# Attention output with the channels on the partitions: y in four column groups of TensorE, without transposes of x

## The chip, the cores and the metric

The kernel runs on one core of one Trainium2 chip. The metric is the device time of one execution, in microseconds (us). A core has TensorE (PE, matrix products), VectorE (DVE), ScalarE (ACT), GpSimd (POOL) and SyncE (SP), which here issues most of the DMA transfers. TensorE writes its products to PSUM; the other operands lie in SBUF. In a product the stationary operand (lhsT) is loaded first, the streamed one (rhs) then runs through, one column after the other, and the output has the columns of lhsT on its partitions. Everything is f32. In the trace an f32 product is two passes, each a weight load and a matmul; a transpose is one.

## The reference

Two blocks stand one behind the other: a linear attention with a decaying state (4 batches, 8 heads, 768 tokens, 48 channels a head), and a feed-forward block over the 3072 rows of 384 channels that it makes.

```python
for t in range(S):                                   # attention, per batch and head
    cur = einsum('bhd,bhe->bhde', u[None] * kt, vt)
    y[:, :, t] = einsum('bhd,bhde->bhe', rt, state + cur)
    state = w[None, :, :, None] * state + einsum('bhd,bhe->bhde', kt, vt)
...
x = y.transpose(0, 2, 1, 3).reshape(B * S, H * D)    # 3072 x 384
h = x @ w_in                                         # 384 -> 1024
e = exp(h - max(h)); sm = e / (sum(e) + 1e-09)
solu = h * sm
ln = (solu - mean) / sqrt(var + 1e-06) * g_ln
out = ln @ w_out                                     # 1024 -> 384
```

## The kernel before

The work is cut into 24 units: six chunks of 128 tokens for each of four batches, chunk by chunk, so that the four batches take turns and a unit finds the state that its batch left four units earlier. Units 0 to 3 are the first chunks and have no state yet; the last four leave none behind.

A unit passes through these functions of `direct_path`:

- `load` (L456): SP fetches k, r and v of the unit into `kpad`, `rpad` (heads padded from 48 to 64 columns) and `vt` (heads of 48 columns, tokens on the partitions; six buffers).
- `weigh` (L601): POOL weighs k into `kp`, and makes the products for the token's own term; ACT writes that term onto the diagonal of `AT`.
- `turn` (L617): TensorE transposes r and k, two heads at a time, to `rT` and `kT` (channels on the partitions, tokens as columns; head pair `a`, `HP` = 4 pairs).
- `scores` (L631): for each head 48 channels by 128 tokens against each other; the two heads of a pair stand in different halves of TensorE's rows. DVE copies what is causal into `AT` (earlier token on the partitions, later token as column).
- `finish` (L644): y of the unit into one PSUM tile `y_ps`, with the tokens on the partitions: four products `rT` by state (L652, stationary `rT`, streamed 96 columns of the state, two heads), then eight products `AT` by `vt` (L657, stationary the scores of a head, streamed its 48 columns of v). ACT copies `y_ps` to `x` (L661). Then k times v (L665) and DVE and POOL bring the state up to date.
- `turn_x` (L674): three transposes of `x`, 128 channels each, to `xt_ps`, and a copy on ACT to `xT` (L680), since the feed-forward block needs the channels on the partitions.
- `ffn_in` (L682): h in two halves of 512 columns into `h_ps` (L687, 12 passes), then max, exp, product and variance on DVE, ACT and POOL.
- `turn_ln` (L709) transposes the normed row (L715), and `ffn_out` (L721) makes the output (L726, 16 passes), which ACT copies and SP writes out.

The order of TensorE's work is written out by hand: the loop at L740 runs under a manual schedule for TensorE alone, and each iteration `i` issues, in this order, the transposes of unit i+2, those of the normed rows of unit i−8, h of unit i−5 (`LA` = 5), the scores of unit i+1, the output of unit i−8 (`LO` = 3 more), y of unit i, and the transposes of x of unit i−4. The other engines' order is the scheduler's. In the first iterations the weights are fetched as pairs of 32-bit words and converted (`convert`, L489) on ACT, DVE and POOL beside the attention. When y has run out, four iterations of the feed-forward block follow that still transpose an x, and then the last outputs.

PSUM: `psM` has four buffers of one bank, shared by all the small tiles (`y_ps`, `kv_ps`, `xt_ps` and so on); `h_ps` has one buffer of two banks, and the scores have two banks.

Of the kernel before, what the change touches and what calls it, by code (L numbers as in the profile page):

```python
# [9 lines left out]
F32 = mybir.dt.float32  # L10
# [386 lines left out]
def direct_path(  # L397
# [184 lines left out]

    def check_range():

        ok = small.tile([1, dm], F32, tag="ok", name="ok")
        ok2 = small.tile([1, dm], F32, tag="ok2", name="ok2")
# [3 lines left out]
        all_ok = small.tile([1, 1], F32, tag="all_ok", name="all_ok")  # L590
# [6 lines left out]
    def pair(t, a):  # L597
        return t[:, 2 * a : 2 * a + 2, :].rearrange("p q d -> p (q d)")
# [42 lines left out]
            nc.vector.copy_predicated(A4[:, :, q, :], later.to_broadcast([128, HP, T]), pss[q])  # L641


    def finish(i):  # L644
        b, c = units[i]
        X = live[i]
        vt, AT, St = vts[i % NV], X["AT"], states[b]
        y_ps = psM.tile([128, H, D], F32, tag="m", name="y_ps")
        first = True
        if c > 0:  # L650
            for a in range(HP):
                nc.tensor.matmul(y_ps[:, 2 * a : 2 * a + 2, :].rearrange("p q d -> p (q d)"),  # L652
                                 X["rT"][:, a, :], St[:, a].rearrange("p q d -> p (q d)"),
                                 start=first, stop=False, skip_group_check=True)
                first = False
        for h in range(H):
            nc.tensor.matmul(y_ps[:, h, :], AT[:, h, :], vt[:, h, :],  # L657
                             start=first, stop=(h == H - 1), skip_group_check=True)
            first = False
        x = X["x"] = fpool.tile([128, dm], F32, name="x", bufs=LA + 1)  # L660
        nc.scalar.copy(out=x, in_=y_ps.rearrange("p h d -> p (h d)"))  # L661
        if c < C - 1:
            kv_ps = psM.tile([128, HP, 2, D], F32, tag="m", name="kv_ps")
            for a in range(HP):
                nc.tensor.matmul(kv_ps[:, a].rearrange("p q d -> p (q d)"),  # L665
                                 pair(X["kp"], a), pair(vt, a), start=True, stop=True)
            if c > 0:
                nc.vector.tensor_add(St, kv_ps, St)
                nc.gpsimd.tensor_mul(St, St, wt)
            else:  # L670
                nc.vector.tensor_mul(St, kv_ps, wt)


    def turn_x(i):  # L674
        X = live[i]
        xt_ps = psM.tile([128, KD, 128], F32, tag="m", name="xt_ps")
        for j in range(KD):
            nc.tensor.transpose(xt_ps[:, j, :], X["x"][:, ts(j, 128)], ident)  # L678
        X["xT"] = fpool.tile([128, KD, 128], F32, name="xT")
        nc.scalar.copy(out=X["xT"], in_=xt_ps)  # L680

    def ffn_in(i):  # L682
        X = live[i]
# [55 lines left out]
    with tc.manual_schedule(engines={mybir.EngineType.PE}):  # L739
        for i in range(-2, N + LA + LO):  # L740
            j, l = i - LA, i - LA - LO
            if 0 <= i and i + 4 < N:
                load(i + 4)
            if 0 <= i + 3 and i + 3 < N and i + 3 >= 2:
                weigh(i + 3)
            if 0 <= i + 2 < N:
                turn(i + 2)
            for _ in range(count.get(i, 1)):
                if i >= -1 and todo:
                    convert(todo.pop(0))  # L750
                if ahead < len(pieces):
                    load_weights(ahead)
                    ahead += 1
            if i == 10:
                check_range()
            if 0 <= l < N and i < N + LA:
                turn_ln(l)
            if 0 <= j < N:
                ffn_in(j)
            if 0 <= i + 1 < N:  # L760
                scores(i + 1)
            if N + LA - 1 <= i < N + LA + LO - 1:
# [50 lines left out]
```

## Time and profile before

| | us |
|---|---|
| median of 3 runs | 456.85 (455.9 to 458.77) |
| the profiled execution: its time | 458.56 |
| the profiled execution: its span, first to last instruction | 456.7 |
| DMA, mean over the span | 57 GB/s |

The profile is one execution. A row such as "256.88 1.91 PE L657 MATMUL ... x16" is 16 instructions of line 657 that begin 256.88 us after the first instruction and end 1.91 us later. The ends of matmuls are modelled and reach into the start of the next, so lengths of stages are best taken from start to start. In a row of the grouped list the numbers behind the bar are the busy time, the mean of one in ns, and the time that the engine stood idle just before such an instruction, with what released it. The granted clock of TensorE was 0.985 of full speed over the span.

### The profile page before, as it was taken

The page shows a single profiled execution, that of the slowest core. Times are in us where ns is not written, and L with a number is a line of the kernel's source. Part 1 is how long each engine was busy: PE and PEld are TensorE (multiplying, and loading weights), DVE is VectorE, ACT ScalarE, POOL GpSimd, SP SyncE. Part 2 cuts the span into 40 slices and gives each one's busy share as a digit, 9 for nine tenths or more (in the row PEclk, how much of TensorE's full clock was granted, in tenths as well). Part 3 has the DMA queues.
Part 4 walks back from the last instruction along what each step waited for, and adds up shares of the span by engine and source line. Part 5 has one row for each costly group of instructions (what it writes and reads, how often), then busy time and mean ns, then how long its engine had stood idle before and what let it go on. Part 6 is the DMA issues. An engine that isn't in the chain of part 4 may idle for free.

```text
span 456.7 us, 5931 instructions
## 1 busy us (share of the span) xinstructions
PE 423.7 (93%) x2221; PEld 289.5 (63%) x2221; DVE 219.5 (48%) x386; ACT 191.2 (42%) x446; POOL 130.9 (29%) x159
## 2 busy tenths in 40 slices
PE   0399897998999999999999999999999999999995
PEld 0398875664766756757757757757756665555562
DVE  5648887987443443443443443533443233333410
ACT  1576578764524524523523523523422233332310
POOL 4447676785223223223223213200000000000000
PEclk9999799999999999999999999999999999999998
DMA  9969949142203203213213101000000000000011
GB/s 156 221 172 180 190 102 195 14 69 52 60 12 70 53 17 69 52 18 70 47 24 69 42 11 37 18 1 17 19 0 19 17 19 17 17 2 17 17 37 40
DMA packets 81587, 25.84 MB, mean 57 GB/s; under 512 B 76557, under 2 KB 79758, under 8 KB 81550
## 3 DMA queue, kind: packets, MB, share of 16 engines
q1 hardware_dynamic: 80364, 25.17, 26.9%
q10 hardware_dynamic: 1186, 0.20, 0.3%
q8 instruction: 19, 0.31, 0.3%
q14 instruction: 18, 0.15, 0.1%
HBM read 20.65 MB, written 4.72 MB: 56 GB/s over the span
## 4 chain that ended last, share of the span: by engine, by line
PE 76%; DVE 11%; ACT 5%; issue 3%; POOL 3%; DMA 1%; ACTq 0%; POOLq 0%
PE h_ps L687 24%; PE o_ps L726 23%; PE y_ps L657 8%; PE at L638 5%; PE t_ps L715 4%; PE kv_ps L665 3%; PE y_ps L652 3%; PE tk_ps L627 2%; PE tr_ps L623 2%; ACT AT L615 1%; DVE solu L697 1%; ACT e L693 1%; PE xt_ps L678 1%; DVE st L691 1%; DVE ma L504 1%
## 5 line engine op out<-in xcount | busy, mean ns | idle before, releaser
L687 PE MATMUL h_ps<-w_in_sb,xT 128*128 128x512 f32 x288 | 129.8, 600 | 2.9 <-DVE solu L697 1.9
L726 PE MATMUL o_ps<-w_out_sb,lnT 128*128 128x384 f32 x384 | 129.2, 490 | 0.0
L726 PEld LDWEIGHTS o_ps<-w_out_sb,lnT 128*128 128x128 f32 x384 | 71.5, 190 | 49.0 <-issue 2.4
L687 PEld LDWEIGHTS h_ps<-w_in_sb,xT 128*128 128x128 f32 x288 | 53.5, 192 | 62.6 <-issue 58.1
L693 ACT ACTIVATE e<-h_ps,st 128x1024 f32<-128x1024 f32 x24 | 26.7, 1113 | 110.8 <-DVE st L691 110.8
L615 ACT ACTIVATE AT<-ident,own 128x128 f32<-128x128 f32 x192 | 60.6, 391 | 10.1 <-DVE own L612 10.0
L702 POOL TENSOR_SCALAR st<-st 128x1 f32<-128x1 f32 x24 | 4.9, 205 | 200.3 <-ACT sq L701 200.2
L691 DVE TENSOR_REDUCE st<-h_ps 128x1 f32<-128x1024 f32 x24 | 29.4, 1223 | 58.9 <-PE h_ps L687 58.9
L657 PE MATMUL y_ps<-vt,AT 128*128 128x48 f32 x384 | 49.5, 285 | 0.0
L657 PEld LDWEIGHTS y_ps<-vt,AT 128*128 128x128 f32 x384 | 48.0, 203 | 0.7 <-issue 0.4
L701 ACT ACTIVATE sq<-solu,st 128x1024 f32<-128x1024 f32 x24 | 27.6, 1149 | 44.3 <-DVE st L699 44.3
L705 DVE TENSOR_SCALAR solu<-solu,st 128x1024 f32<-128x1024 f32 x24 | 21.6, 899 | 50.0 <-POOL st L704 47.5
L605 POOL TENSOR_TENSOR kp<-kpad,kdec 128x512 f32<-128x512 f32 x24 | 30.8, 1287 | 43.3 <-PE kv_ps L665 40.4
L638 PEld LDWEIGHTS at<-rT,kT 48*128 48x128 f32 x384 | 25.7, 200 | 18.0 <-issue 13.9
L641 DVE COPY_PREDICATED AT<-later,at 128x512 f32<-128x512 uint32 x48 | 32.7, 726 | 3.0 <-PE at L638 3.0
L638 PE MATMUL at<-rT,kT 48*128 48x128 f32 x384 | 31.0, 300 | 2.4 <-DVE AT L641 2.4
L612 DVE TENSOR_REDUCE own<-rku 128x8 f32<-128x384 f32 x24 | 13.1, 548 | 38.2 <-POOL rku L610 38.2
L610 POOL TENSOR_TENSOR rku<-rku,rpad 128x384 f32<-128x384 f32 x24 | 24.5, 1021 | 23.4 <-DMA rpad<-in_r_dram 22.8
L697 DVE SCALAR_TENSOR_TENSOR solu<-h_ps,st,e 128x1024 f32<-128x1024 f32 x24 | 30.8, 1283 | 0.8
L609 POOL TENSOR_TENSOR rku<-kpad,u_bc 128x384 f32<-128x384 f32 x24 | 26.2, 1093 | 8.4 <-DMA kpad<-in_k_dram 5.5
L661 ACT COPY x<-y_ps 128x384 f32<-128x384 f32 x24 | 11.4, 476 | 38.5 <-PE y_ps L657 38.5
L715 PE MATMUL t_ps<-ident,solu 128*128 128x128 f32 x192 | 25.2, 273 | 2.0 <-DVE st L699 1.9
(67 smaller groups left out, 424.2 us busy)
## 6 DMA issues: line engine op xcount, KB each, us to landing
kpad<-in_k_dram SPq DMA_DIRECT2D x24, 192.0 KB, 4.2
rpad<-in_r_dram SPq DMA_DIRECT2D x24, 192.0 KB, 4.9
vt<-in_v_dram SPq DMA_DIRECT2D x24, 192.0 KB, 3.0
out_dram<-o SPq DMA_DIRECT2D x24, 192.0 KB, 1.9
raw<-in_moe_w_in_dram SPq DMA_DIRECT2D x6, 512.0 KB, 5.2
raw<-in_moe_w_out_dram SPq DMA_DIRECT2D x8, 384.0 KB, 3.4
u_bc<-in_u_dram ACTq DMA_DIRECT2D x1, 192.0 KB, 3.7
g_sb<-in_moe_g_ln_dram ACTq DMA_DIRECT2D x1, 4.0 KB, 5.6
```

The lines of the kernel that those rows point to most:

```text
L605: nc.gpsimd.tensor_mul(kp.rearrange("p h d -> p (h d)"), kt.rearrange("p h d -> p (h d)"), kdec.rearrange("p a d -> p (a d)"))
L615: nc.scalar.activation(out=AT[:, h, :], in_=ident, func=ACT.Copy, scale=own[:, h])
L638: nc.tensor.matmul(pss[q][:, a, :], X["kT"][rows, a, :], X["rT"][rows, a, :], start=True, stop=True)
L641: nc.vector.copy_predicated(A4[:, :, q, :], later.to_broadcast([128, HP, T]), pss[q])
L657: nc.tensor.matmul(y_ps[:, h, :], AT[:, h, :], vt[:, h, :], start=first, stop=(h == H - 1), skip_group_check=True)
L687: nc.tensor.matmul(h_ps[:, ts(n, NX)], X["xT"][:, j, :], w_in_sb[:, j, ts(n, NX)], start=(j == 0), stop=(j == KD - 1))
L691: nc.vector.tensor_reduce(out=nmax, in_=h_ps, axis=AX.X, op=ALU.max, negate=True)
L693: nc.scalar.activation(out=e, in_=h_ps, func=ACT.Exp, bias=nmax, accum_out=se)
L697: nc.vector.scalar_tensor_tensor(out=solu, in0=h_ps, scalar=rs, in1=e, op0=ALU.mult, op1=ALU.mult, accum_out=tot)
L701: nc.scalar.activation(out=sq, in_=solu, func=ACT.Square, bias=nmu, accum_out=ss)
L715: nc.tensor.transpose(t_ps[:, f, :], X["solu"][:, ts(4 * g + f, 128)], ident)
L726: nc.tensor.matmul(o_ps, X["lnT"][:, f, :], w_out_sb[:, f, :], start=(f == 0), stop=(f == KF - 1))
```

## The change

y is computed with the channels on the partitions, so that it can be used by `ffn_in` as it stands. The operands change places: the state and v become the stationary side, cut into pieces of 32 channels, and `rT` and the scores the streamed side, 128 tokens at a time. The 384 channels are 12 pieces; piece `m` goes to partitions 32·(m mod 4) and on, of column block m div 4 of `y_ps`. A piece that straddles two heads of a pair (every third) is made of two products: `vt` gets 32 zero columns behind each head's 48, and each of the two products takes 32 columns of which 16 are zeros. So there are 12 products with the state and 16 with the scores, ordered so that consecutive ones go to partition groups 0, 1, 2, 3 in turn. ACT copies `y_ps` straight to `xT`, which now has six buffers; `x`, its transposes and the second copy are gone, and `turn_x` is no longer called. Four small constants get one buffer each in place of four, and POOL clears the new columns of `vt` once at the start.

```diff
-    vts = [const.tile([128, H, D], F32, name=f"vt{i}") for i in range(NV)]
+    vts = [const.tile([128, H, D + 32], F32, name=f"vt{i}") for i in range(NV)]
...
+    for vt in vts:
+        nc.gpsimd.memset(vt[:, :, D:], 0.0)
...
-    mf = small.tile([128, T], F32, tag="mf", name="mf")
+    mf = small.tile([128, T], F32, tag="mf", name="mf", bufs=1)
...
+    def parts(m):
+        a, n = divmod(m, 3)
+        at = {0: [(0, 0)], 1: [(0, 32), (1, 64)], 2: [(1, 96)]}[n]
+        return [(2 * a + q, a * 2 * (D + 32) + off) for q, off in at]
+
+    inner = [[(m,) + p for m in range(g, 12, 4) for p in parts(m)] for g in range(4)]
+    inner = [group[n] for n in range(4) for group in inner]
...
-        y_ps = psM.tile([128, H, D], F32, tag="m", name="y_ps")
-        first = True
+        vf = vt.rearrange("p h d -> p (h d)")
+        y_ps = psM.tile([128, KD, 128], F32, tag="m", name="y_ps")
+        last = {m: n for n, (m, h, at) in enumerate(inner)}
+        opened = set()
+
+        def into(m, lhsT, rhs, stop):
+            j, g = divmod(m, 4)
+            nc.tensor.matmul(y_ps[32 * g : 32 * g + 32, j, :], lhsT, rhs, start=(g not in opened),
+                             stop=stop, skip_group_check=True)
+            opened.add(g)
+
         if c > 0:
-            for a in range(HP):
-                nc.tensor.matmul(y_ps[:, 2 * a : 2 * a + 2, :].rearrange("p q d -> p (q d)"),
-                                 X["rT"][:, a, :], St[:, a].rearrange("p q d -> p (q d)"),
-                                 start=first, stop=False, skip_group_check=True)
-                first = False
-        for h in range(H):
-            nc.tensor.matmul(y_ps[:, h, :], AT[:, h, :], vt[:, h, :],
-                             start=first, stop=(h == H - 1), skip_group_check=True)
-            first = False
-        x = X["x"] = fpool.tile([128, dm], F32, name="x", bufs=LA + 1)
-        nc.scalar.copy(out=x, in_=y_ps.rearrange("p h d -> p (h d)"))
+            for m in range(12):
+                a, n = divmod(m, 3)
+                into(m, St[:, a].rearrange("p q d -> p (q d)")[:, ts(n, 32)], X["rT"][:, a, :],
+                     False)
+        for n, (m, h, at) in enumerate(inner):
+            into(m, vf[:, at : at + 32], AT[:, h, :], last[m] == n)
+        X["xT"] = fpool.tile([128, KD, 128], F32, name="xT", bufs=LA + 1)
+        nc.scalar.copy(out=X["xT"], in_=y_ps)
         if c < C - 1:
...
-                                 pair(X["kp"], a), pair(vt, a), start=True, stop=True)
+                nc.tensor.matmul(kv_ps[:, a], pair(X["kp"], a), vt[:, 2 * a : 2 * a + 2, 0:D],
+                                 start=True, stop=True)
...
-    def turn_x(i):
-        X = live[i]
-        xt_ps = psM.tile([128, KD, 128], F32, tag="m", name="xt_ps")
-        for j in range(KD):
-            nc.tensor.transpose(xt_ps[:, j, :], X["x"][:, ts(j, 128)], ident)
-        X["xT"] = fpool.tile([128, KD, 128], F32, name="xT")
-        nc.scalar.copy(out=X["xT"], in_=xt_ps)
...
-            if 0 <= j + 1 < N:
-                turn_x(j + 1)
```

More of the change, by code (lines that the diff above doesn't have):

```diff
@@ L583, in check_range @@
     def check_range():
-        ok = small.tile([1, dm], F32, tag="ok", name="ok")
-        ok2 = small.tile([1, dm], F32, tag="ok2", name="ok2")
+        ok = small.tile([1, dm], F32, tag="ok", name="ok", bufs=1)
+        ok2 = small.tile([1, dm], F32, tag="ok2", name="ok2", bufs=1)
         nc.vector.tensor_single_scalar(out=ok, in_=wrow, scalar=LOW, op=ALU.is_ge)
@@ L589, in check_range @@
         nc.vector.tensor_mul(ok, ok, ok2)
-        all_ok = small.tile([1, 1], F32, tag="all_ok", name="all_ok")
+        all_ok = small.tile([1, 1], F32, tag="all_ok", name="all_ok", bufs=1)
         nc.vector.tensor_reduce(out=all_ok, in_=ok, axis=AX.X, op=ALU.min)
@@ L664, in finish @@
             for a in range(HP):
-                nc.tensor.matmul(kv_ps[:, a].rearrange("p q d -> p (q d)"),
-                                 pair(X["kp"], a), pair(vt, a), start=True, stop=True)
+                nc.tensor.matmul(kv_ps[:, a], pair(X["kp"], a), vt[:, 2 * a : 2 * a + 2, 0:D],
+                                 start=True, stop=True)
             if c > 0:
```

## The prediction

> **What bounds the kernel now.** I read the page's first lines and slices first, then the busy time by stretches, then TensorE's timeline of one iteration.
>
> ```profile
> span 456.7 us, 5931 instructions
> PE 423.7 (93%) x2221; PEld 289.5 (63%) x2221; DVE 219.5 (48%) x386; ACT 191.2 (42%) x446; POOL 130.9 (29%) x159
> PE   0399897998999999999999999999999999999995
> ...
> ```
> ```profile
> 30.00:63.00 33.00, 30.64 (x227) 28.77 (x227) 26.14 (x41) 19.96 (x50) 21.35 (x18) 0.90 0.89 167
> 63.00:118.30 55.30, 49.71 (x276) 32.42 (x275) 45.10 (x74) 36.47 (x88) 36.20 (x38) 0.97 0.42 76
> 118.30:373.40 255.10, 255.10 (x1395) 174.64 (x1393) 106.33 (x183) 99.11 (x230) 55.20 (x72) 1.00 0.15 34
> 373.40:456.70 83.30, 76.91 (x269) 43.95 (x268) 23.98 (x43) 22.19 (x42) 3.71 (x10) 0.98 0.06 20
> ```
>
> The columns of the second fence are the stretch, its length, then the busy time of PE, weight loads, DVE, ACT and POOL. From 118.3 to 373.4 us TensorE is busy for all of the 255.10 us, while DVE has 106 and ACT 99: there every nanosecond taken off TensorE comes off the time, and every one added is paid. Between 63 and 118 us TensorE is idle for 5.6 us and DVE is busy for 45 of 55: the conversion of the weights stands beside it. After 373 us 6.4 us of TensorE are idle.
>
> One iteration of the full stretch, TensorE alone (start, duration, and how many passes; an f32 product is two passes, a transpose one):
>
> ```profile
> 249.66 1.16 PE L638 MATMUL at<-rT,kT 48*128 48x128 f32 x16
> 250.75 5.43 PE L726 MATMUL o_ps<-w_out_sb,lnT 128*128 128x384 f32 x16
> 256.01 1.03 PE L652 MATMUL y_ps<-state,rT 128*128 128x96 f32 x8
> 256.88 1.91 PE L657 MATMUL y_ps<-vt,AT 128*128 128x48 f32 x16
> 258.62 1.10 PE L665 MATMUL kv_ps<-vt,kp 128*128 128x96 f32 x8
> 259.56 0.49 PE L678 MATMUL xt_ps<-ident,x 128*128 128x128 f32 x3
> 259.89 0.60 PE L623 MATMUL tr_ps<-ident,rpad 128*128 128x128 f32 x4
> ...
> 260.76 1.04 PE L715 MATMUL t_ps<-ident,solu 128*128 128x128 f32 x8
> 261.63 5.32 PE L687 MATMUL h_ps<-w_in_sb,xT 128*128 128x512 f32 x12
> 266.88 1.16 PE L638 MATMUL at<-rT,kT 48*128 48x128 f32 x16
> ```
>
> The ends overlap the next starts (matmuls are pipelined), so I count from start to start: the iteration is 266.88 − 249.66 = 17.22 us. Of it y takes 258.62 − 256.01 = 2.61 us for 24 passes and the transposes of x 259.89 − 259.56 = 0.33 us for 3. That is the part the change replaces: 2.94 us.
>
> **What the change puts there.** Per unit with a state: 12 products of a 32-column piece of the state with rT, and 16 of a 32-column piece of vt with the scores, 28 products or 56 passes, each streaming 128 columns; they go round four column groups of 32. What one such pass costs alone the trace shows at full width: eight passes that stream 128 columns (L715) take 261.63 − 260.76 = 0.87 us, 0.109 us each. y now streams 48 columns and its 16 passes take 1.74 us, also 0.109 each, so there the 128-column weight load is the limit and not the streaming. The change exchanges a short stream and a wide load for a long stream and a narrow load; with one pass at a time it would lose: 56 × 0.109 = 6.10 us in place of 2.94. It wins only if the column groups run beside each other.
>
> No instruction of this trace has a column group. The bounds of one round of four passes are therefore 0.109 us (four at once cost what one does) and 4 × 0.109 = 0.436 us (one after the other). The nearest row is L638: there two heads stand in two row groups, and 16 passes with 128 streamed columns take 250.75 − 249.66 = 1.09 us, where one after the other they would need 16 × 0.109 = 1.74. They do run beside each other, although each head's two passes follow each other in the program. So I take the lower end: 56 / 4 = 14 rounds × 0.109 = 1.53 us.
>
> **The price of changing the grouping.** L638 also shows what entering and leaving such a grouping costs, in iterations with and without it:
>
> ```profile
> 345.03 5.32 PE L687 MATMUL h_ps<-w_in_sb,xT 128*128 128x512 f32 x12
> 350.28 1.16 PE L638 MATMUL at<-rT,kT 48*128 48x128 f32 x16
> 351.37 5.43 PE L726 MATMUL o_ps<-w_out_sb,lnT 128*128 128x384 f32 x16
> 356.63 1.03 PE L652 MATMUL y_ps<-state,rT 128*128 128x96 f32 x8
> ...
> 360.46 5.32 PE L687 MATMUL h_ps<-w_in_sb,xT 128*128 128x512 f32 x12
> 365.62 5.32 PE L726 MATMUL o_ps<-w_out_sb,lnT 128*128 128x384 f32 x16
> 370.78 1.03 PE L652 MATMUL y_ps<-state,rT 128*128 128x96 f32 x8
> ```
>
> h_ps takes 5.25 us ahead of the scores and 5.16 ahead of o_ps; o_ps takes 5.26 behind the scores and 5.16 behind h_ps: 0.10 on either side. Inside, 8 rounds × 0.109 = 0.87 leave 1.09 − 0.87 = 0.22 us. One excursion costs 0.42 us, and y has none today. It lies on TensorE, so it is paid. Bounds: 0 and twice that; I take 0.42.
>
> So y becomes 1.53 + 0.42 = 1.95 us for 2.94: 0.99 us less. Units 8 to 23 finish in the full stretch: 16 × 0.99 = **15.8 us**.
>
> **The tail.** Four iterations after the last y have a transpose of x alone:
>
> ```profile
> 386.00 0.48 ACT L680 COPY xT<-xt_ps 128x384 f32<-128x384 f32 x1
> 386.53 5.42 PE L687 MATMUL h_ps<-w_in_sb,xT 128*128 128x512 f32 x12 [0.24 <-ACT xT L680]
> 391.78 5.32 PE L726 MATMUL o_ps<-w_out_sb,lnT 128*128 128x384 f32 x16
> 396.94 0.49 PE L678 MATMUL xt_ps<-ident,x 128*128 128x128 f32 x3
> 398.54 1.98 PE L687 MATMUL h_ps<-w_in_sb,xT 128*128 128x512 f32 x4 [0.23 <-ACT xT L680]
> ```
>
> They last 398.54 − 386.53 = 12.01 us: h_ps waits for the copy L680, which stands behind other ACT work. With neither transpose nor copy there remain t_ps 0.87, h_ps 5.16 and o_ps 5.16, 11.19 us: 4 × 0.82 = **3.3 us**. What is late next there is nothing near: solu of the unit is due three iterations later.
>
> **The first 118 us.** Units 0 to 3 have no state and no transpose in their iteration: 16 passes at 0.109 = 1.74 us become 32 passes, 8 rounds, 0.87 + 0.42 = 1.29. Units 4 to 7 gain 0.99 each. In all 4 × 0.45 + 4 × 0.99 = 5.8 us less work, but the chain of waits leaves TensorE between 64 and 106 us:
>
> ```profile
> 66.19 1.35 POOL kp L605
> ...
> 71.46 2.45 ACT AT L615 x8
> ...
> 77.19 0.36 ACT xT L680
> ...
> 104.34 1.29 DVE solu L697 x2
> ```
>
> There the saved time turns into longer waits. The copies of x lie on ACT, which is on that chain, and one of two goes. Bounds 0 and 5.8; I take **2**, near the lower end, because the chain is elsewhere.
>
> **What costs nothing, and why.**
>
> ```profile
> 0.78 0.20 POOL masks.py:197 MEMSET ident<- 128x128 f32 x1 [0.29 <-POOLq L797]
> 1.65 0.42 POOL L574 MEMSET wt<- 128x384 f32 x1
> 5.41 1.58 SPq L460 DMA_DIRECT2D vt<-in_v_dram  x1
> 6.01 1.19 POOL L609 TENSOR_TENSOR rku<-kpad,u_bc 128x384 f32<-128x384 f32 x1 [3.94 <-DMA kpad<-in_k_dram]
> L661 ACT COPY x<-y_ps 128x384 f32<-128x384 f32 x24 | 11.4, 476 | 38.5 <-PE y_ps L657 38.5
> ```
>
> - Six memsets of 128x256 on POOL, at most 0.42 us each by the wt row, 2.5 us: they push ident back, but POOL then idles 3.94 us before L609, and the first load into vt is issued at 5.41 us, after them. If that cover were gone they would cost 2.5 us once.
> - ACT copies y_ps to xT at the same size as x before, and the second copy goes: 11.4 us of ACT, which nothing waits for in the full stretch.
> - The v loads write to a pitch of 80 instead of 48; a row of a head is 192 bytes either way, so the packets stay. kv_ps streams 96 columns as before. Buffers of constants drop from four to one; each is used once.
> - xT now has six buffers as x had; it is read five iterations after it is written.
>
> **The sum.** 15.8 + 3.3 + 2 = 21.1 us. The profiled execution took 458.56 us, 456.7 of it span, and lies 1.7 us above the median of 456.85. It would take 437.5; against the median, 435.8, and I write 436.
>
> **A page's price.** The Trainium skill, "TensorE: Matmul & The Clock Gate", Part 3 (measured speedup), gives 2.38 times for three column groups at M=32, N=512, that is 0.79 of ideal; at that share four groups give 3.17 times, an estimate from that page: 56 × 0.109 / 3.17 + 0.42 = 2.35 us, and a sum of some 14 us in place of 21 (443). Against its four row groups at 3.07 times, L638 of this trace does better once the 0.22 us are set apart, so I stay with the full factor.
>
> **The rivals.**
>
> 1. *Two abreast.* Each round costs 0.218 us, because only as much runs at once as the trace shows, two: 28 × 0.109 + 0.42 = 3.47 us, 0.53 more than today. 16 × 0.53 = 8.5, less the tail's 3.3; early units +0.53 and (3.47 and 2.16 for 2.94 and 1.74) +0.42, 3.8, half of it hidden: +7.1, **464 us, slower**. For it: two passes in 0.109 us is the fastest feed of TensorE in this trace, and whether four column groups can be fed 128 rows each at once no row shows. Against it: L638 has no sign of a limit by the feed; its rounds are as long as one pass. It decides from a round of 0.18 us on ((2.94 − 0.42) / 14).
>
> 2. *The loads no longer hide.* Today a load runs under the pass before it. If a column group's load had to wait until the array is free, a round would be one pass and four loads; a 128-column load fills 0.109 us at L657, so 32 columns are 0.027 by width: 0.109 + 4 × 0.027 = 0.218, again 3.47 us and **464 us**; more if a load does not shrink with its width. The same skill page (Part 3, what overlaps) says that loads overlap matmuls in flight only where row groups differ, and column groups share all rows. Against it in this trace:
>
> ```profile
> L687 PEld LDWEIGHTS h_ps<-w_in_sb,xT 128*128 128x128 f32 x288 | 53.5, 192 | 62.6 <-issue 58.1
> ```
>
> h_ps loads full height under a pass of full height, 192 ns each, and 12 passes still take 5.16 us, which leaves nothing for loads between them.
>
> 3. *One at a time.* The grouping does nothing: 6.10 + 0.42 = 6.52 us, +3.58 × 16 = 57.3; tail −3.3; units 4 to 7 +14.3 less 5.6 of idle; units 0 to 3 (32 × 0.109 + 0.42 − 1.74) × 4 = +8.7: +71, **528 us**. L638 speaks against it.
>
> 4. *Between three and four abreast*, or a feed that holds for part of the burst: half way to rival 1, **450 us**.
>
> **How the numbers follow.** Four abreast 0.60; rival 4 0.13; rivals 1 and 2 0.08 each; rival 3 0.11. The time is that of the likeliest, 436. Its own range is 425 (no excursion cost, all of the early gain: −0.42 × 16 − 3.8) to 443 (twice the excursion cost: +0.42 × 16). For 8 in 10 the range goes on to rivals 1, 2 and 4: 425 to 466, and leaves out rival 3. About 1% is what a measurement of this kernel can tell from no change (452.3 to 461.4). Faster: 0.60 and most of rival 4, 0.70; same: 0.07; slower: rivals 1 and 2 for the most part and rival 3, 0.23.
>
> **What the profile afterwards would show.** Right: y's 56 passes start to start in about 1.95 us, an iteration of 16.2 us in the full stretch, still without TensorE idle; h_ps to h_ps 11.2 us in the tail; o_ps ahead of y 0.10 us longer. Wrong: y at 3.5 us (rivals 1 and 2; under rival 2 with gaps between rounds that loads fill) or at 6.5 (rival 3). If y is short but the iteration is not, another engine has become the bound, and idle time would stand before TensorE's lines.

## The result, and the profile after

| | before | after |
|---|---|---|
| median of the runs, us | 457.81 (455.9 to 465.57) | 435.9 (434.72 to 436.09) |
| profiled execution: time, us | 458.56 | 434.72 |
| profiled execution: span, us | 456.7 | 433.0 |

The kernel became faster: the ratio is 0.9529, with a 95% interval of 0.9486 to 0.9573. The fourth run of the kernel before, 465.57 us, is a slow one and is left out of the ratio; the median of the other three is 456.85 us. Predicted were 436.0 us.

First the page of the changed kernel, its opening lines:

```profile
span 433.0 us, 7179 instructions
PE 386.2 (89%) x2853; PEld 244.0 (56%) x2853; DVE 214.7 (50%) x386; ACT 181.6 (42%) x422; POOL 133.2 (31%) x165
PE   0178692878999999999999999999999999999994
```

TensorE lost 423.7 − 386.2 = 37.5 us of busy time, but the span only 23.7. The slices show why: nine tenths or more now begin in the eleventh slice (a slice is 10.8 us), and the first hundred microseconds have sevens, a six and a two where they had mostly eights and nines before. Part of the work that went had not been on the path.

Busy time by stretches (stretch, length, then PE, weight loads, DVE, ACT, POOL), cut where y of unit 8 begins and where the last y ends:

```profile
30.00:63.00 33.00, 27.14 (x354) 21.22 (x352) 28.23 (x46) 23.50 (x63) 22.16 (x20) 1.00 0.90 167
63.00:116.10 53.10, 39.72 (x345) 24.62 (x344) 39.41 (x68) 31.53 (x75) 34.00 (x37) 0.94 0.42 72
116.10:353.10 237.00, 237.00 (x1861) 149.17 (x1860) 104.41 (x183) 93.34 (x215) 54.91 (x72) 1.00 0.17 36
```

TensorE is still busy for all of the full stretch, which is now 237.00 us long (255.10 before): no other engine has become the bound there. Between 63 and 116 us it now idles 53.10 − 39.72 = 13.4 us, before 55.30 − 49.71 = 5.6.

One iteration of the full stretch, TensorE alone (start, duration, passes):

```profile
238.23 1.16 PE L640 MATMUL at<-rT,kT 48*128 48x128 f32 x16
239.32 5.43 PE L737 MATMUL o_ps<-w_out_sb,lnT 128*128 128x384 f32 x16
244.68 0.86 PE L668 MATMUL y_ps<-rT,state 128*32 128x128 f32 x24
245.36 1.06 PE L668 MATMUL y_ps<-AT,vt 128*32 128x128 f32 x32
246.35 1.13 PE L684 MATMUL kv_ps<-vt,kp 128*128 128x96 f32 x8
247.32 0.60 PE L625 MATMUL tr_ps<-ident,rpad 128*128 128x128 f32 x4
...
254.31 0.94 PE L640 MATMUL at<-rT,kT 48*128 48x128 f32 x12
```

Start to start, y takes 246.35 − 244.68 = 1.67 us for 56 passes; the transposes of x are gone. The iteration is 254.31 − 238.23 = 16.08 us, it was 17.22. o_ps ahead of y takes 5.36 us (0.10 more than before) and kv_ps behind it 0.97 (0.03 more).

How many passes of y are on TensorE at a time is seen by cutting the same view into pieces of 0.11 us and looking at y alone (busy time, and in brackets how many passes are in flight):

```profile
244.66:244.80 0.14, 0.12 (x4) 1.00 0.00 0
244.80:244.91 0.11, 0.11 (x8) 1.00 0.00 0
244.91:245.02 0.11, 0.11 (x12) 1.00 0.00 0
```

Each of the first three pieces has four more than the one ahead of it. A pass is in flight for some 0.27 us (its end is modelled), so from the third piece on 12 touch each piece. Four start in every 0.109 us: that is four abreast, with a round of 0.109 us.

The tail, in the same columns as the iteration:

```profile
365.23 5.32 PE L698 MATMUL h_ps<-w_in_sb,xT 128*128 128x512 f32 x12
...
376.41 5.32 PE L698 MATMUL h_ps<-w_in_sb,xT 128*128 128x512 f32 x12
```

An iteration here is 376.41 − 365.23 = 11.18 us (12.01 before), and h_ps waits for nothing.

So the 23.7 us of span come from three places: 16 iterations × 1.14 = 18.2 in the full stretch; 4 × 0.82 = 3.3 in the tail; and unit 8's y, with which the full stretch begins, starts at 116.1 us instead of 118.3, 2.2. The profiled execution of the changed kernel had TensorE's granted clock at 1.00 between 30 and 63 us, that of before 0.90; the other three runs of the changed kernel have spans of 434.0 to 434.4 us at mean clocks of 0.973 to 0.977 (0.991 here). About 1 us of the 2.2 may belong to that and not to the change.

### The profile page after: what moved, and what is told of

Its sections match the earlier page's. It is cut to its first block, busy times and chain, and to the rows that moved or that the text cites. A ratio compares the mean times of both kernels' runs of the same rounds, so it can differ in the third digit from the quotient of the medians.

```text
span 433.0 us, 7179 instructions
## 1 busy us (share of the span) xinstructions
PE 386.2 (89%) x2853; PEld 244.0 (56%) x2853; DVE 214.7 (50%) x386; ACT 181.6 (42%) x422; POOL 133.2 (31%) x165
## 4 chain that ended last, share of the span: by engine, by line
PE 77%; POOL 8%; DVE 6%; issue 3%; ACT 2%; SPq 2%; DMA 1%; POOLq 0%; ACTq 0%; DVEq 0%
PE o_ps L737 29%; PE h_ps L698 27%; PE y_ps L668 7%; PE t_ps L726 5%; PE at L640 4%; PE kv_ps L684 3%; POOL kp L607 3%; POOL rku L612 2%; PE tr_ps L625 1%; POOL rku L611 1%; PE tk_ps L629 1%; DMA rpad<-in_r_dram 1%; DVE AT L643 1%; ACT AT L617 1%; SPq L462 1%
## 5 line engine op out<-in xcount | busy, mean ns | idle before, releaser
L617 ACT ACTIVATE AT<-ident,own 128x128 f32<-128x128 f32 x192 | 59.1, 391 | 8.3 <-DVE own L614 8.3
L640 PEld LDWEIGHTS at<-rT,kT 48*128 48x128 f32 x384 | 24.7, 189 | 22.9 <-issue 15.5
L640 PE MATMUL at<-rT,kT 48*128 48x128 f32 x384 | 30.0, 287 | 7.0 <-DVE AT L643 6.7
L612 POOL TENSOR_TENSOR rku<-rku,rpad 128x384 f32<-128x384 f32 x24 | 25.1, 1050 | 18.2 <-DMA rpad<-in_r_dram 17.5
L668 PE MATMUL y_ps<-AT,vt 128*32 128x128 f32 x768 | 25.5, 273 | 0.0
L726 PEld LDWEIGHTS t_ps<-ident,solu 128*128 128x128 f32 x192 | 21.7, 141 | 5.2 <-issue 2.2
L684 PE MATMUL kv_ps<-vt,kp 128*128 128x96 f32 x160 | 22.6, 284 | 0.8 <-DVE state L690 0.8
```

Of the source, the lines that this page charges most:

```text
L612: nc.gpsimd.tensor_mul(rku, rku, rt[:, :, 0:D])
L617: nc.scalar.activation(out=AT[:, h, :], in_=ident, func=ACT.Copy, scale=own[:, h])
L640: nc.tensor.matmul(pss[q][:, a, :], X["kT"][rows, a, :], X["rT"][rows, a, :], start=True, stop=True)
L668: nc.tensor.matmul(y_ps[32 * g : 32 * g + 32, j, :], lhsT, rhs, start=(g not in opened), stop=stop, skip_group_check=True)
L684: nc.tensor.matmul(kv_ps[:, a], pair(X["kp"], a), vt[:, 2 * a : 2 * a + 2, 0:D], start=True, stop=True)
L726: nc.tensor.transpose(t_ps[:, f, :], X["solu"][:, ts(4 * g + f, 128)], ident)
```

## The experiments

The questions were: is it the column groups, as priced, that shorten y (and not, say, a feed that happens to be fast enough); what did the transposes and the copy of x cost by themselves; and why did the first stretch give so little, where 5.8 us of TensorE's work went by the prediction and more by the trace. Each run below is compared with runs of the kernel before that were taken beside it; their medians lie between 455.5 and 457.2 us, so a difference of a microsecond between two experiments is not told from none.

**Only the pitch and the zero columns, on the kernel before** (e1). y stays as it was.

```diff
-    vts = [const.tile([128, H, D], F32, name=f"vt{i}") for i in range(NV)]
+    vts = [const.tile([128, H, D + 32], F32, name=f"vt{i}") for i in range(NV)]
...
+    for vt in vts:
+        nc.gpsimd.memset(vt[:, :, D:], 0.0)
...
-            nc.tensor.matmul(y_ps[:, h, :], AT[:, h, :], vt[:, h, :],
+            nc.tensor.matmul(y_ps[:, h, :], AT[:, h, :], vt[:, h, 0:D],
...
```

> The kernel before with only the wider vt (pitch 80), the six memsets on POOL and the single buffers of the constants; y and the transposes of x as before. Theory (these parts are hidden): 457 us, within 1% of the kernel before, y stage still 2.6 us and x transposes 0.33 us. Rival (the wider pitch or the memsets at the start cost something): up to 2.5 us more, seen as a later first product on TensorE, or longer landings of vt.

Measured: 463.98 us, ratio 1.0184 (1.0113 to 1.0255). This was not expected: the part that was to cost nothing, or 2.5 us by the rival, costs 6.8 us by the medians (its profiled execution was the fastest of four, 461.57 us). TensorE's stages are the same (an iteration is 17.22 us), but unit 8's y starts at 121.3 us, 3.0 later than before; the profiled span lost no more than that (459.8 for 456.7). VectorE's rows of this run, 13 to 18 us (start, duration):

```profile
13.22 0.17 DVE L557 TENSOR_TENSOR tab<-tab,pw 128x8 f32<-128x8 f32 x1
13.30 0.42 DVE L502 TENSOR_SCALAR mag<-mag 128x512 f32<-128x512 f32 x1
13.64 0.17 DVE L557 TENSOR_TENSOR tab<-tab,pw 128x16 f32<-128x16 f32 x1
```

and the same place in the kernel before:

```profile
13.86 3.85 DVE L555 TENSOR_TENSOR tab<-tab,pw 128x8 f32<-128x8 f32 x7
```

The seven steps that build the decay table `tab` ran in one go before; now steps of the weights' conversion (L502 here, more behind it) stand between them. DVE is not touched by the edit. The order of the engines other than TensorE is the scheduler's, and it came out another way, on ACT and POOL too. The first transposes that wait for the table start 0.8 us later (18.56 for 17.76); where the rest of the 3.0 us arises was not followed.

**The same without the zero columns** (e7): pitch and single buffers alone.

```diff
-    vts = [const.tile([128, H, D], F32, name=f"vt{i}") for i in range(NV)]
+    vts = [const.tile([128, H, D + 32], F32, name=f"vt{i}") for i in range(NV)]
...
-    mf = small.tile([128, T], F32, tag="mf", name="mf")
+    mf = small.tile([128, T], F32, tag="mf", name="mf", bufs=1)
...
```

> The kernel before with the wider vt (pitch 80) and the single buffers, but without the six memsets; the zero columns are not read there. Every engine has the same instructions in the same order as in the kernel before. Theory (what cost time in the pitch-only kernel is not the pitch: the memsets made the scheduler place the weight conversion between the steps of the table on DVE): 457 us, within 1% of the kernel before, first transpose of the table at 17.8 us. Rival (the transfers into the wider pitch are slower): 460 us or more, as in the pitch-only kernel.

Measured: 457.86 us, ratio 1.0014 (0.9984 to 1.0045). `tab` is built in one go again, and DVE, ACT and POOL have the order of the kernel before throughout:

```profile
14.03 3.88 DVE L555 TENSOR_TENSOR tab<-tab,pw 128x8 f32<-128x8 f32 x7
```

So the pitch and the buffers are free, and what e1 lost hangs on the six memsets, through the order.

**The changed kernel with the memsets written later** (e8), behind the first two calls of `weigh`:

```diff
-    for vt in vts:
-        nc.gpsimd.memset(vt[:, :, D:], 0.0)
...
     weigh(0)
     weigh(1)
+    for vt in vts:
+        nc.gpsimd.memset(vt[:, :, D:], 0.0)
```

> The changed kernel with the six memsets written behind the first two units' weighing, still on POOL; by this DVE's first forty instructions stand in the order of the kernel before. Theory (the memsets' place disturbs the start by the order of DVE and POOL): 3 to 6 us less than the changed kernel, 430 to 433 us, the first transpose of the table at 17.8 and not 19.1 us. Rival (the start's loss is caught up in the stretch that the conversions bound): 435 to 436 us.

Measured: 433.36 us, ratio 0.9494 (0.9465 to 0.9524): 2.5 us under the changed kernel by the medians, 1.6 by the ratios, 1.5 by the spans of the profiled executions. The direction is as expected, the amount is smaller than the 3 to 6 us of the theory, and the intervals of the two ratios overlap. The rows of this run:

```profile
11.80 1.57 POOL L749 MEMSET vt<- 128x256 f32 x6
14.25 3.80 DVE L555 TENSOR_TENSOR tab<-tab,pw 128x8 f32<-128x8 f32 x7
18.11 1.12 PE L561 MATMUL kd_ps<-ident,tab 128*128 128x128 f32 x4 [10.53 <-DVE tab L555]
114.61 0.86 PE L666 MATMUL y_ps<-rT,state 128*32 128x128 f32 x24
```

against those of the changed kernel:

```profile
19.07 1.11 PE L563 MATMUL kd_ps<-ident,tab 128*128 128x128 f32 x4 [11.54 <-DVE tab L557]
...
116.08 0.86 PE L668 MATMUL y_ps<-rT,state 128*32 128x128 f32 x24
```

The table is made in one go, the first transposes that wait for it start 1.0 us sooner, and unit 8's y 1.5 us sooner. The memsets themselves take the same 1.57 us; only their place in the program has changed.

**The same products, one column group after the other** (e3). Each product is what it was; only the order in the program differs.

```diff
-    inner = [group[n] for n in range(4) for group in inner]
+    inner = [x for group in inner for x in group]
...
-            for m in range(12):
+            for m in [m for g in range(4) for m in range(g, 12, 4)]:
```

> The changed kernel with the 12 and the 16 products ordered by column group: all of group 0, then all of 1, 2 and 3, so that neighbours in the program stand in the same group; same work. Theory (every column group works off its own passes, and TensorE's queue hands out passes that stand behind others that wait): y stays near 1.7 us and the time near 436 us. Rival (passes start in program order, so that only neighbours in different groups overlap): 56 x 0.109 = 6.1 us of y, 4.4 us more in 16 iterations and part of it in the earlier ones: 510 to 530 us.

Measured: 464.18 us, ratio 1.0161 (1.0094 to 1.0228): slower than before. y takes 3.38 us, neither the 1.7 of one theory nor the 6.1 of the other. The passes of y in flight at the start of one y and near its end:

```profile
206.95:207.09 0.14, 0.12 (x1) 1.00 0.00 0
207.09:207.20 0.11, 0.11 (x2) 1.00 0.00 0
207.20:207.31 0.11, 0.11 (x4) 1.00 0.00 0
...
210.00:210.11 0.11, 0.11 (x3) 1.00 0.00 0
```

Where the changed kernel has 4, 8 and 12, here one pass starts, then another, then two; at the end three are in flight, which is one in each round. So the order in the program decides how many groups run together. TensorE's rows of this y, up to kv behind it:

```profile
206.97 1.26 PE L668 MATMUL y_ps<-rT,state 128*32 128x128 f32 x20
207.97 0.30 PE L668 MATMUL y_ps<-AT,vt 128*32 128x128 f32 x1
208.04 0.30 PE L668 MATMUL y_ps<-rT,state 128*32 128x128 f32 x2
...
210.36 1.13 PE L684 MATMUL kv_ps<-vt,kp 128*128 128x96 f32 x8
```

All products with the state stand ahead of those with the scores in the program. Yet the first pass of `AT` starts at 207.97 us, before the last passes of the state at 208.04: a pass of an idle group goes past waiting passes of a busy one, but only some way.

**Two groups at a time** (e4): first groups 0 and 1 in turn, then 2 and 3.

```diff
-    inner = [group[n] for n in range(4) for group in inner]
+    inner = [inner[g][n] for k in (0, 2) for n in range(4) for g in (k, k + 1)]
...
-            for m in range(12):
+            for m in [4 * n + g for k in (0, 2) for n in range(3) for g in (k, k + 1)]:
```

> The changed kernel with the products ordered so that groups 0 and 1 take turns first and 2 and 3 afterwards; same work. Theory (queue hands out what can run, whatever the order): y near 1.7 us, 436 us. Rival (only neighbours overlap): two abreast, 28 x 0.109 + 0.14 = 3.2 us of y, 1.5 us more in 16 iterations and some more before: about 463 us.

Measured: 443.68 us, ratio 0.9712 (0.9647 to 0.9777). y takes 2.13 us, again between the two theories. TensorE's rows, and the passes in flight in the same y:

```profile
200.82 0.89 PE L668 MATMUL y_ps<-rT,state 128*32 128x128 f32 x20
...
202.95 1.13 PE L684 MATMUL kv_ps<-vt,kp 128*128 128x96 f32 x8
```

```profile
200.80:200.94 0.14, 0.12 (x2) 1.00 0.00 0
200.94:201.05 0.11, 0.11 (x4) 1.00 0.00 0
201.05:201.16 0.11, 0.11 (x8) 1.00 0.00 0
...
201.27:201.38 0.11, 0.11 (x12) 1.00 0.00 0
...
202.70:202.81 0.11, 0.11 (x6) 1.00 0.88 321
```

It begins two abreast, is four abreast after two rounds, and ends two abreast.

**Half as long streams, twice as many passes** (e5): each product in two halves of 64 columns, 112 passes.

```diff
-            nc.tensor.matmul(y_ps[32 * g : 32 * g + 32, j, :], lhsT, rhs, start=(g not in opened),
-                             stop=stop, skip_group_check=True)
-            opened.add(g)
+            for s in range(2):
+                nc.tensor.matmul(y_ps[32 * g : 32 * g + 32, j, ts(s, 64)], lhsT, rhs[:, ts(s, 64)],
+                                 start=(g not in opened), stop=stop, skip_group_check=True)
+                opened.add(g)
```

> The changed kernel with each product of y in two, 64 of the 128 tokens each: 112 passes a unit of half the length, every weight load done twice, same result. Theory (a round lasts as long as its stream, the loads of 32 columns and the handing out of passes have room to spare): 28 rounds of 0.055 us, y stays near 1.7 us and the time near 436 us. Rival (TensorE is already handed its passes as fast as it can be, one in 0.027 us, or the load of a group needs the whole 0.109 us): 28 x 0.109 + 0.14 = 3.2 us of y, 1.5 us more in 16 iterations and some more before: about 463 us.

Measured: 440.4 us, ratio 0.9642 (0.9594 to 0.969). The y stage:

```profile
216.99 0.89 PE L669 MATMUL y_ps<-rT,state 128*32 128x64 f32 x46
...
218.76 0.46 PE L685 MATMUL kv_ps<-vt,kp 128*128 128x96 f32 x2
```

112 passes, each with its own load, take 218.76 − 216.99 = 1.77 us, 0.016 us each; 56 take 1.67. Handing out passes is therefore no limit to y at 56. The whole is nevertheless 4.5 us slower than the changed kernel: 16 × 0.10 = 1.6 of that is y, and unit 8's y starts at 119.9 us in place of 116.1. The first stretch has another order on DVE, ACT and POOL from some 40 us on; why it is this much later was not followed up.

**The transposes and the copy back, with the new y** (e2):

```diff
+    def turn_x(i):
+        X = live[i]
+        xt_ps = psM.tile([128, KD, 128], F32, tag="m", name="xt_ps")
+        for j in range(KD):
+            nc.tensor.transpose(xt_ps[:, j, :], X["xT"][:, j, :], ident)
+        X["xx"] = fpool.tile([128, KD, 128], F32, name="xx")
+        nc.scalar.copy(out=X["xx"], in_=xt_ps)
...
+            if 0 <= j + 1 < N:
+                turn_x(j + 1)
```

> The changed kernel with three 128x128 transposes of its xT and their copy on ACT put back where the transposes of x stood; the feed-forward block reads the transposed blocks, so its numbers are those of another x. Theory (most of the gain is y itself, run four abreast): the transposes cost 16 x 0.33 in the full stretch, 4 x 0.82 in the tail and about 1 us at the start, 9.6 us more than the changed kernel: 445 us, the iteration 16.08 + 0.33 = 16.41 us. Rival (the gain is mostly the missing transposes and copies): 450 us or more, close to the kernel before.

Measured: 447.46 us, ratio 0.9785 (0.9733 to 0.9838), 11.6 us more than the changed kernel and between the two theories; the iteration is 16.40 us, as the first had it. By the spans it is 446.6 − 433.0 = 13.6: 16 iterations × 0.33 = 5.3; the tail's four by 0.83, 3.3; and unit 8's y at 121.2 us, 5.1 later. h_ps in one of these tail iterations:

```profile
376.35 5.42 PE L706 MATMUL h_ps<-w_in_sb,xx 128*128 128x512 f32 x12 [0.23 <-ACT xx L699]
```

The wait of h_ps for the copy on ACT is back as it stood before the change. So 5.3 + 3.3 = 8.6 us of the gain come not from y but from what y's new form makes unnecessary. Whether the 5.1 us at the start belong to it too, the next two runs leave open.

**The copy alone** (e11) and **the transposes alone, read by nothing** (e12):

```diff
+    def turn_x(i):
+        X = live[i]
+        X["xx"] = fpool.tile([128, KD, 128], F32, name="xx")
+        nc.scalar.copy(out=X["xx"], in_=X["xT"])
...
+            if 0 <= j + 1 < N:
+                turn_x(j + 1)
```

> The changed kernel with a copy of xT on ACT where the transposes of x stood, read by the feed-forward block, and no transposes; same result. In the run with transposes and copy put back the full stretch began 5.1 us later than in the changed kernel (121.2 for 116.1 us). Theory (that loss is the copy's, in ACT's queue on the chain of the conversions): the full stretch begins at 120 us or later, its iteration stays 16.08 us, 440 us. Rival (it is the transposes', or their two together): it begins near 116 us, 436 to 437 us.

```diff
+    def turn_x(i):
+        X = live[i]
+        xt_ps = psM.tile([128, KD, 128], F32, tag="m", name="xt_ps")
+        for j in range(KD):
+            nc.tensor.transpose(xt_ps[:, j, :], X["xT"][:, j, :], ident)
...
+            if 0 <= j + 1 < N:
+                turn_x(j + 1)
```

> The changed kernel with the three transposes of xT where those of x stood, and no copy; nothing reads them. Theory (the loss at the start is the copy's): the full stretch begins near 117 us, its iteration is 16.40 us, and the tail is 4 x 0.33 us longer: 442 to 443 us. Rival (it is the transposes'): it begins at 120 us or later, 446 us.

Measured: with the copy 435.42 us, ratio 0.9544 (0.9499 to 0.9588), no different from the changed kernel, as the rival had it; unit 8's y starts at 116.7 us. The copy by itself costs nothing. With the transposes 444.49 us, ratio 0.974 (0.9695 to 0.9785), 8.6 us more and between the two theories. The transposes cost 16 × 0.33 = 5.3 us in the full stretch and some 1.3 in the tail, and unit 8's y starts at 118.7 us, 2.6 later. The other 2.0 us of e2's tail come only when transpose and copy stand in one chain ahead of h_ps.

The start cannot be divided in the same way. e7, whose engines have the order of before, has its unit 8 at 117.7 us where before has 118.3, so 0.6 us there is nothing. In e2 and e12 the order of DVE, ACT and POOL departs from the changed kernel's from some 63 us on, in e11 it does not. And e5, with neither transposes nor copy but with another order, has its unit 8 at 119.9 us. So the later start of e2 and e12 may be the transposes' or the order's.

**The scores moved beside y** (e6), so that TensorE changes its grouping once and not twice in an iteration. In e6 the call stands behind the output of unit i−8 instead of ahead of it.

```diff
             if 0 <= j < N:
                 ffn_in(j)
-            if 0 <= i + 1 < N:
-                scores(i + 1)
...
             if 0 <= l < N:
                 ffn_out(l)
+            if 0 <= i + 1 < N:
+                scores(i + 1)
```

> The changed kernel with the scores of the next unit issued behind the output product, directly ahead of y, so that TensorE goes from rows in two groups straight to columns in four; same work. Theory (each change of the grouping costs some 0.1 us and more on TensorE, and there is one less): the iteration 0.1 to 0.3 us shorter, 2 to 5 us in all, 431 to 434 us. Rival (the passage between two groupings costs as much as the passage to and from none, or the later scores make the masked copy late): no change or slower.

Measured: 432.14 us, ratio 0.9459 (0.9421 to 0.9496), 3.8 us less than the changed kernel, as expected. One iteration:

```profile
200.51 5.32 PE L698 MATMUL h_ps<-w_in_sb,xT 128*128 128x512 f32 x12
205.66 5.32 PE L737 MATMUL o_ps<-w_out_sb,lnT 128*128 128x384 f32 x16
210.92 1.16 PE L640 MATMUL at<-rT,kT 48*128 48x128 f32 x16
212.01 0.86 PE L668 MATMUL y_ps<-rT,state 128*32 128x128 f32 x24
...
213.68 1.13 PE L684 MATMUL kv_ps<-vt,kp 128*128 128x96 f32 x8
...
216.39 3.17 PE L698 MATMUL h_ps<-w_in_sb,xT 128*128 128x512 f32 x7
```

h_ps now takes 5.15 us (5.25 ahead of the scores) and o_ps 5.26 (5.36 when it stood between scores and y); the scores and y keep their 1.09 and 1.67. The iteration is 216.39 − 200.51 = 15.88 us. Going straight from row groups to column groups costs no more than going to either from full width, and one way in and one way out, 0.1 us each, are saved.

**Both: memsets later and scores beside y** (e9), on the changed kernel:

```diff
-    for vt in vts:
-        nc.gpsimd.memset(vt[:, :, D:], 0.0)
...
     weigh(1)
+    for vt in vts:
+        nc.gpsimd.memset(vt[:, :, D:], 0.0)
...
-            if 0 <= i + 1 < N:
-                scores(i + 1)
...
+            if 0 <= i + 1 < N:
+                scores(i + 1)
```

> The changed kernel with both: the scores directly ahead of y, and the memsets behind the first two units' weighing. Theory (the one acts in the full stretch, the other in the first 115 us, so they add): 0.19 us an iteration off as in the run with the scores beside y, 2 us at the start: 429.5 to 431 us. Rival (the start's gain is lost again in the conversions' stretch): 432 us, as with the scores alone.

Measured: 430.73 us, ratio 0.9457 (0.9433 to 0.9482), within what was expected. The trace has both gains: the iteration is 15.88 us as in e6, and unit 8's y starts at 114.3 us, near e8's 114.6. In the times the second gain is hardly seen: 1.4 us less than e6 by the medians, and by the ratios (0.9459 there) nothing.

**k times v in column groups too** (e10), on top of e9: the product per pair made 128 by 96 (two heads, padded to 64 channels, by two of 48), of which only the two diagonal blocks are the state's; now each head is one product of 64 output partitions, the two heads of a pair in two groups.

```diff
-                nc.tensor.matmul(kv_ps[:, a], pair(X["kp"], a), vt[:, 2 * a : 2 * a + 2, 0:D],
-                                 start=True, stop=True)
+                for q in range(2):
+                    nc.tensor.matmul(kv_ps[q * P : (q + 1) * P, a, q, :], X["kp"][:, 2 * a + q, :],
+                                     vt[:, 2 * a + q, 0:D], start=True, stop=True,
+                                     skip_group_check=True)
+            for q in range(2):
+                rows = slice(q * P, (q + 1) * P)
+                if c > 0:
+                    nc.vector.tensor_add(St[rows, :, q, :], kv_ps[rows, :, q, :], St[rows, :, q, :])
...
+    for t in states:
+        nc.gpsimd.memset(t, 0.0)
```

> As the run before, and the product of k and v cut by heads: eight products of 64 stationary columns in two column groups in place of four of 128, each streaming 48 columns; the state is added to by halves on DVE, and cleared once by POOL. Theory (the stage is bound by 128-column loads, 0.109 us a pass; loads of half the width in two groups beside each other take half of that, and y has paid for entering column groups already): kv 0.44 to 0.6 us in place of 0.97, 6 to 9 us less in 20 iterations, 421 to 425 us. Rival (passing from four groups to two and to none costs as much as it brings, or the longer adds on DVE hold the state back): 430 us or more.

Measured: 426.08 us, ratio 0.9349 (0.9325 to 0.9374), the fastest of all. From one iteration:

```profile
209.03 0.67 PE L683 MATMUL kv_ps<-vt,kp 128*64 128x48 f32 x16
209.64 0.66 PE L623 MATMUL tr_ps<-ident,rpad 128*128 128x128 f32 x4
```

kv takes 0.61 us where it took 0.97, the stage behind it 0.05 more, and the iteration is 15.57. It came out 1 us above what was expected: the gain of 15.88 − 15.57 = 0.31 us falls in the 12 iterations of the full stretch whose unit leaves a state, 3.7 us, and the first stretch gave almost none (unit 8's y at 114.0 us, e9 114.3).

## Why the prediction was right

**The number: closer than its terms.** The sum was worked out for the profiled execution: 21.1 us off, 437.5 us. The profiled executions give 23.7 us off the span and 434.72 us, so the sum was 2.6 us short, nearly all of it in the full stretch. That the medians came to 435.9 where 436 was written is luck: the profiled execution of before lies 1.7 us above its median, that of the changed kernel 1.2 below. The mechanism and the time of y are what the runs bear out.

**Four abreast: right.** The forecast stood on rounds of 0.109 us with four passes each, taken from rows in which only two ran together. The rows in flight, 4, 8, 12, show it, and e3 and e4 show that it is the column groups that do it: the same passes in another order take 3.38 and 2.13 us. The price by the Trainium skill, "TensorE: Matmul & The Clock Gate", Part 3, from its 2.38 times for three column groups, gave 2.35 us for y with its surroundings and 443 us; the trace has 1.80 us, of which y itself is 1.67, and 435.9. Here the four groups give all of their factor; what is lost lies at the ends of the stage.

**The price of changing the grouping: too high.** It was the one term of the sum that was mis-sized: 0.42 us, borrowed from the scores. Measured: o_ps ahead 0.10 longer, kv behind 0.03 longer, and inside 1.67 − 1.53 = 0.14, together 0.27. The stage with its surroundings is 1.80 us instead of 1.95, which over 16 iterations is 2.4 us: the full stretch gave 18.2 us where 15.8 were forecast. (The forecast's list of signs has 1.95 us for y from start to start; by its own terms that part is 1.53 + 0.22 = 1.75.) That the way in and the way out are real and paid is shown by e6, which takes one of each away and gains 0.2 us in an iteration. The Trainium skill, "TensorEngine Tiling (Array Packing)", Key Properties, says that a change of tiling mode drains TensorE; it gives no time, and these rows fit it with about 0.1 us on the way in and as much on the way out.

**The tail: exact,** 3.3 us forecast and measured, for the reason given: the wait of h_ps for the copy is gone, and nothing near is late next. e2 brings that wait back.

**The first stretch: the number came out by luck.** 2 us were forecast and 2.2 measured, but these are a gain less a loss. The forecast named "six memsets of 128x256 on POOL" under what costs nothing, with 2.5 us as the most. That step failed. Their own time is small and hidden, as it said (1.57 us in all), but adding them changed the scheduler's order on DVE: e1 shows a loss of 6.8 us for memsets and pitch on the old kernel, e7 none for the pitch alone, and e8 regains 1.5 to 2.5 us in the new kernel by placing them later. The saved work did turn into waits, as forecast: at 77 us an h_ps waits 8.78 us for DVE in the changed kernel; the one at that place before waited 1.20. TensorE's row of the changed kernel (the wait in brackets):

```profile
76.90 6.96 PE L698 MATMUL h_ps<-w_in_sb,xT 128*128 128x512 f32 x12 [8.78 <-DVE solu L708]
```

and of the kernel before:

```profile
78.27 7.02 PE L687 MATMUL h_ps<-w_in_sb,xT 128*128 128x512 f32 x12 [1.20 <-DVE solu L697]
```

What shortens the first stretch was not settled. With the transposes back it ends at 118.7 to 121.2 us (e12, e2), and e2, with the new y, is no earlier than e1, with the old one (121.3); but e5, without transposes, is at 119.9, and in all four the other engines have an order of their own. Which work of DVE and POOL makes it late after 19 us was not settled either.

**ACT's copy and the pitch cost nothing: right.** e11 (the copy back: no change) and e7 (the pitch: no change).

**The rivals.** Two abreast (464 us) and one at a time (528) are excluded by the rows in flight; loads that do not hide (464) by the rounds: with four passes started in every 0.109 us no place is left for a load. The rule beside that rival (the Trainium skill, "TensorE: Matmul & The Clock Gate", Part 3), that loads overlap only where the row groups differ, does not hold here: all four column groups share all rows. A limit by the feed of the streamed rows is excluded by the same rounds; e5, with a pass every 0.016 us, shows that the handing out and the loads do not bound them either. The rivals' time itself was met once, by e3 at 464.18 us, for another reason: the same change with the products in another order would have been the slower kernel.

## What to carry to other kernels

Products with few output partitions can be set side by side in column groups at the full factor (here f32, 32 columns, 128 streamed), if consecutive products in the program go to different groups; the order is as important as the placement. Look for an orientation in which the result lies as its reader wants it: what falls away behind the product (here 8.6 us at least) can be worth as much as the product. And where a scheduler orders the other engines, an added instruction that is hidden by its duration can still cost several microseconds through the order; compare the order of the untouched engines before believing "free".

## What the runs showed of the hardware that was not expected

TensorE seems to hold back passes by column group. The numbers of y by program order, 1.67, 2.13 and 3.38 us for 4, 2 and 1 groups in turn, come near a simple picture: passes are handed out in the order of the program, one group runs one pass per 0.109 us, and about three passes can wait for a busy group before everything behind them waits too. Counted by hand from the first start to the last round's end, three waiting passes give 14, 18 and 28 rounds, 1.53, 1.96 and 3.05 us, which is 0.14, 0.17 and 0.33 less than measured; two would give 3.82 for the last, four 2.51. The picture is inferred from these three orders and was not tested by itself; that passes start out of the program's order is shown by the rows of e3.

A load shrinks less than its width; rival 2 had assumed in proportion. The loads of y by their tile, in the changed kernel (duration in ns: shortest, median, longest):

```profile
L668 PEld LDWEIGHTS y_ps<-AT,vt x768: 106/110/110, 30.9 to 352.8; 128*32 128x32 f32 x192
```

and in the kernel before:

```profile
L657 PEld LDWEIGHTS y_ps<-vt,AT x384: 186/192/333, 29.6 to 373.2; 128*128 128x128 f32 x192
```

A quarter of the columns takes 110 / 192 = 0.57 of the time (kv in e10, with half of them, 138 ns). It stays hidden all the same, for the loads of a round run beside each other. It need not even be as short as a round: in e5 the loads take the same 110 ns, the rounds 1.77 / 28 = 0.063 us.

What entering and leaving cost is seen in the starts of single passes in the trace of the changed kernel. On the way in, y's first pass starts 0.415 us behind o_ps's last, where the passes of o_ps are 0.322 apart, and the first round lasts 0.134 us in place of 0.109. On the way out, kv's first pass starts 0.20 us behind y's last, where only 0.09 separate the last pass of a round from the first of the next. So most of the 0.14 us inside y is the way out. The scores leave their row groups with the same 0.20 us. Behind them o_ps has 0.427 us between its first two passes, 0.10 more than later; behind y kv has 0.187, 0.04 more than in the kernel before.
